# Putting off the feed-forward layer of 896 tokens behind the attention, as Strassen units of 448 tokens

## The chip, the core and the metric

The kernel runs on one core of a Trainium2 chip. The core has a matrix engine (TensorE, PE in the profile; PEld is its weight load), a vector engine (VectorE, DVE), a scalar engine (ScalarE, ACT), a general engine (GpSimd, POOL) and SyncE (SP), which here only issues DMAs. Each engine works through its own instructions in order; semaphores hold them to each other. The metric is the device time of one execution in microseconds (us), lower is better: the median of the runs shown, beside one execution that the hardware profiler recorded.

## What is computed

Softmax attention over 8 batches of 12 heads (448 positions of 64), and then a gated feed-forward layer (FFN) on all 3584 tokens:

```python
scores = scale * np.matmul(q, k.transpose(0, 1, 3, 2))
scores = scores - np.max(scores, axis=-1, keepdims=True)
attn = np.exp(scores)
attn = attn / (np.sum(attn, axis=-1, keepdims=True) + 1e-09)
attn_out = np.matmul(attn, v)
x = attn_out.transpose(0, 2, 1, 3).reshape(B * S, H * D)      # 3584 x 768
g = x @ w_gate                                                # 768 x 1536
silu = g * (1.0 / (1.0 + np.exp(-g)))
val = x @ w_val                                               # 768 x 1536
out = silu * val @ w_out                                      # 1536 x 768
```

All inputs and outputs are float32; the kernel multiplies in float16.

## The kernel before

**Attention.** Heads are taken in pairs (48 pairs, 6 per batch). For a pair, GpSimd's queue loads queries, keys and values, GpSimd copies them into order (L237), and from pair 12 on two DMA transposes on SP's queue (L239, L243) bring queries and keys into `qkT`. The scores of a chunk are matmuls into a PSUM tile `s` (L329; L341 for the chunk that two pairs share), ScalarE takes their exponential into `E` (L349), and 32 matmuls per pair (L420) multiply by the values: `pv_rest` has the first 8 of them, `pv_pieces` the other 24. `pv_close` divides by the sums on DVE (L449, L450), and `turn_x` transposes the result into `X` with two more DMA transposes on SP (L494, L498). `X[kk]` holds the 896 tokens of batches 2kk and 2kk+1; there are two such buffers.

**PSUM.** Three double tiles (`ps_s`) are shared in rotation by scores, gates, output groups and units. Two single tiles (`ps_f`) are shared by attention products, values and plain outputs.

**FFN in steps.** While attention runs, the tokens go through the FFN in blocks: block 2kk has 384 tokens, block 2kk+1 has 512. A block has 12 `Step`s, one per 128 columns of the hidden layer: 6 gate matmuls, tanh on ScalarE (L584), 6 value matmuls, and on DVE two instructions (L610, L616) that write `hts`. `run_single` splits the value product of a lone step into two halves, `run_pair` interleaves two steps.

**Outputs.** Two chunks of 128 tokens make a pair for a seven-product (Strassen) scheme: `out_group` (L679) has 42 matmuls of 192 columns for half of the output columns. Its first half makes three products, which DVE combines (L718 or ScalarE's L720, then L721 and L723); the second half begins with a product that adds to what L723 wrote. DVE prepares the sums of `hts` (`h_sums`). A third chunk of a 384-token block goes plainly, in four parts of 192 columns (L650).

**The visits.** The attention's order is a `plan` of visits. Each has three score chunks and, mostly, the products of one earlier pair. From the visit `base` on, a table says what each does beside them: `(begins, nf, ng, no, ns)` are the block that begins, the number of steps, output groups, plain output parts, and extra sums on DVE. There are 33 visits. If a visit has one group and no step, `around` is set: `run_group_with` puts the attention products inside the group. No entry of the table before sets it.

**Behind the last exponential.** The last four batches' remainder is worked off as Strassen units. Block 5 (512 tokens of batches 4 and 5) goes in units of 256, and batches 6 and 7 in units of 448. A `Unit` takes 256 hidden columns of gate or value and two token halves with seven products of 3 matmuls each (L795); there are 12 units. It needs four sums of weights, made on GpSimd (`weight_sums`, L758 to L761), and four sums of tokens (`token_sums`). `order_of` fixes the order of a run of units by estimated durations. Then come the output groups of block 4 and block 5, the second run of units, one chunk of 128 tokens alone (`single_out`, L1003), and three pairs of groups.

Of the kernel before, what the change touches and what calls it, by code (L numbers as in the profile page):

```python
# [17 lines left out]
NB = 2  # L18
# [46 lines left out]
def kernel(  # L65
# [818 lines left out]
    with tc.manual_schedule():  # L884
# [63 lines left out]
        def add_block(i, visits):  # L948
            if i < B - NB - 1:
                f1, own, n = block(i)  # L950
                fvq.extend(f1)
                kk, c0, hts = own
            else:
                own = None
# [12 lines left out]
            groups.extend(x for t in range(1 + odd) for x in pair_groups(kk, c0, hts, t))  # L967
# [121 lines left out]

        def run_group_with(p0):  # L1090
# [6 lines left out]

        def run_two_groups(inside=None):
            gens = [groups.pop(0)[0]() for _ in range(2)]
            for stage in range(2):  # L1100
                for gen in gens:
                    next(gen)
                if inside and not stage:
                    inside()
# [92 lines left out]
        hts5 = hview(384, 512)  # L1197
        vfree = vraw[:].rearrange("p s h c d -> p (s h c d)")
        VE = 2 * NC * D
        t5 = token_space(vfree[:, 3 * VE :], 256)  # L1200
        for x, (chunks, todo) in enumerate(plan):
# [40 lines left out]
            around = bool(todo) and x > base and VISITS[x - base][1:3] == (0, 1)  # L1242
            for _, p0 in todo if not around else []:
                pv(p0)
                if p0 < XPE:
                    turns.append(p0)
                else:
                    turn_x(p0)
# [22 lines left out]
            else:  # L1271
# [6 lines left out]
                if around:  # L1278
                    run_group_with(todo[0][1])
                elif ng:  # L1280
# [17 lines left out]
                if x == len(VISITS) + base - 6:  # L1298
                    space = raws_all[:, 0 : RL // 2].rearrange("p a t b x -> p (a t b x)")
                    wsum_space(space, 10)  # L1300
# [3 lines left out]
                    wsum_space(vfree, 4)  # L1304
            if x == len(VISITS) + base - 6:
                tsums5 = token_sums(X[KL - 1][:, :, 384:], 256, t5)
            if len(VISITS) + base - 6 <= x < len(VISITS) + base - 2:
                tsums5.pop(0)()
            for u in {len(VISITS) + base - 6: range(4), len(VISITS) + base - 2: range(4, 6)}.get(x, []):
                weight_sums(u)  # L1310
            while turns:
                turn_x(turns.pop(0))
        x5 = X[KL - 1][:, :, 384:]
# [50 lines left out]
        units = {}  # L1364
        items = unit_items(units, lambda u: Unit(u, 256, x5, t5, hts5), 256)
        p0 = NPAIR - 1
        pv_open(p0, True)
        pv_rest(p0)
        pv_quad(p0)
        turn_x(p0)  # L1370

        wsum_space(Eall[:, 4 * NK * 128 : ER * EC], 18)
        wsum_space(attp.tile([128, 2 * S + D], FP16, tag="qkT", name="wsum", bufs=QB), 2)
        for vo in Vts[:4]:
            wsum_space(vo[:].rearrange("p h c d -> p (h c d)"), 1)
        for u in range(6, NFB):
            items[f"W_{u}"] = (POOL_, 3.65, [f"W_{u - 1}"], lambda u=u: weight_sums(u))
# [81 lines left out]
```

## Time and profile before

| | us |
|---|---|
| median of 3 runs (429.52 to 430.11) | 429.69 |
| span of the profiled execution | 428.2 |
| first unit matmul (L795) | 300.98 |
| groups of blocks 4 and 5 end, second run of units begins | 351.35 |
| second run of units ends | 399.72 |
| last group matmul ends | 424.1 |

The page cuts the span into 40 slices of 10.7 us and gives the busy share of each in tenths (9 is 90% or more):

```profile
PE   8999999999999999999999999999999999999996
ACT  6975667556566645546667556568655225545221
POOL 8756543999887583658543885934999000000001
PEclk9999999999999999999999999999999999999999
DMA  9999999999999999999999999823100331000125
```

A busy PE is one whose matmuls are pipelined and whose ends are modelled, so a 9 hides idle time of some tenths of a microsecond; these show in the chain and in the instructions in order of time. The DMA row counts engines that have packets under way, and several queues can share an engine.

### The profile page before, as it was taken

How to read it: one execution, taken by the hardware profiler on the slowest of the kernel's cores; microseconds unless marked ns; L12 is line 12 of the kernel's file. 1: busy time of each engine (PE TensorE's matmuls, PEld its weight loads, DVE VectorE, ACT ScalarE, POOL GpSimd, SP SyncE). 2: the span in 40 equal slices, each digit the busy share in tenths (PEclk: the TensorE clock that was granted, in tenths of full speed). 3: DMA queues.
4: the chain of work that ended last, by engine and by line, in shares of the span. 5: the costliest groups of instructions: out<-in, count | busy, mean ns of one | idle time of the engine just before them, and what ended most of it. 6: DMA issues, size and time to landing. Idle time of an engine off the chain costs nothing.

```text
span 428.2 us, 11621 instructions
## 1 busy us (share of the span) xinstructions
PE 420.5 (98%) x4635; PEld 290.2 (68%) x4635; DVE 267.7 (63%) x642; ACT 245.2 (57%) x395; POOL 233.3 (54%) x358
## 2 busy tenths in 40 slices
PE   8999999999999999999999999999999999999996
PEld 3666656555557777747666677777888995555795
DVE  4666562576758665575545776567777765565663
ACT  6975667556566645546667556568655225545221
POOL 8756543999887583658543885934999000000001
PEclk9999999999999999999999999999999999999999
DMA  9999999999999999999999999823100331000125
GB/s 138 177 200 200 199 173 190 121 169 209 160 138 137 115 146 150 146 136 120 124 151 122 139 149 117 152 45 97 25 1 14 101 99 51 0 0 2 38 76 148
DMA packets 108551, 50.02 MB, mean 117 GB/s; under 512 B 60864, under 2 KB 105232, under 8 KB 108496
## 3 DMA queue, kind: packets, MB, share of 16 engines
q0 software_dynamic: 46944, 24.83, 54.0%
q1 hardware_dynamic: 61408, 24.27, 33.6%
q8 instruction: 36, 0.59, 0.7%
q14 instruction: 19, 0.16, 0.1%
q10 hardware_dynamic: 144, 0.17, 0.1%
HBM read 49.55 MB, written 11.01 MB: 141 GB/s over the span
## 4 chain that ended last, share of the span: by engine, by line
PE 77%; DMA 15%; POOL 4%; DVE 1%; ACT 1%; issue 1%; SPq 0%; POOLq 0%; DVEq 0%
PE og L679 18%; PE gp L557 15%; PE un L795 10%; PE vp L557 9%; PE acc L420 8%; PE ub L795 8%; PE s L329 5%; DMA wv<-in_moe_w_val_dram 4%; DMA qkraw<-in_q_dram 4%; DMA qkraw<-in_k_dram 3%; DMA wg<-in_moe_w_gate_dram 2%; PE op L650 2%; POOL qkraw L200 2%; DMA qkT<-qk 1%; PE s L341 1%; PE op L1003 1%
## 5 line engine op out<-in xcount | busy, mean ns | idle before, releaser
L349 ACT ACTIVATE E<-s 128x896 f16<-128x896 f32 x126 | 106.6, 918 | 40.2 <-PE s L329 28.2
L557 PE MATMUL gp<-X,wg 128*128 128x384 f16 (+1 forms) x360 | 73.9, 347 | 0.0
L237 POOL COPY qk<-qkraw 128x512 f16<-128x512 f16 x72 | 43.7, 649 | 50.8 <-DMA qkT<-qk 48.9
L557 PE MATMUL vp<-X,wv 128*128 128x384 f16 (+3 forms) x360 | 66.7, 321 | 0.1
L610 DVE SCALAR_TENSOR_TENSOR t<-sg,gp 128x384 f32<-128x384 f32 (+1 forms) x60 | 36.3, 607 | 42.5 <-ACT sg L584 42.2
L557 PEld LDWEIGHTS <-wv 128*128 128x128 f16 x462 | 43.8, 98 | 25.8 <-issue 0.3
L640 POOL DMA_DIRECT2D out_dram<-osb x3 | 1.6, 541 | 90.9 <-ACT osb L698 90.9
L177 POOL DMA_DIRECT2D vraw<-in_v_dram x72 | 43.8, 629 | 12.8 <-DVE X L492 6.9
L557 PEld LDWEIGHTS <-wg 128*128 128x128 f16 x360 | 32.8, 98 | 26.1 <-issue 1.9
L584 ACT ACTIVATE sg<-gp 128x384 f32<-128x384 f32 (+1 forms) x60 | 32.1, 537 | 28.8 <-PE gp L557 28.1
L177 POOL DMA_DIRECT2D qkraw<-in_k_dram x70 | 42.4, 619 | 7.7 <-DMA wo<-in_moe_w_out_dram 4.7
L367 ACT ACTIVATE E<-s 112x896 f16<-112x896 f32 x48 | 40.5, 919 | 8.5 <-PE s L359 8.3
L420 PEld LDWEIGHTS <-E 128*128 128x128 f16 (+1 forms) x1152 | 37.4, 96 | 10.9 <-issue 4.7
L679 PEld LDWEIGHTS <-hts 128*128 128x128 f16 x528 | 44.1, 98 | 0.3
L420 PE MATMUL acc<-vo,E 128*128 128x65 f16 (+1 forms) x1152 | 42.3, 192 | 0.7 <-DVE X L492 0.3
L616 DVE SCALAR_TENSOR_TENSOR hts<-t,vp 128x384 f16<-128x384 f32 (+3 forms) x60 | 32.5, 541 | 5.5 <-PE vp L557 1.9
L698 ACT ACTIVATE osb<-og 128x384 f32<-128x384 f32 x22 | 10.8, 491 | 39.4 <-PE og L679 37.5
L200 POOL DMA_DIRECT2D qkraw<-in_q_dram x44 | 29.9, 680 | 5.4 <-DMA vraw<-in_v_dram 1.4
L450 DVE TENSOR_TENSOR xt<-acc,R 128x256 f16<-128x256 f32 x72 | 30.6, 425 | 2.5
L329 PE MATMUL s<-qkT 64*128 64x448 f16 x216 | 30.4, 354 | 0.6 <-DMA qkT<-qk 0.5
L679 PE MATMUL og<-wo,hts 128*128 128x192 f16 x264 | 29.0, 246 | 0.0
L679 PEld LDWEIGHTS <-hsum 128*128 128x128 f16 x300 | 25.5, 98 | 1.0
(180 smaller groups left out, 723.8 us busy)
## 6 DMA issues: line engine op xcount, KB each, us to landing
vraw<-in_v_dram POOLq DMA_DIRECT2D x72, 64.0 KB, 4.9
qkraw<-in_q_dram POOLq DMA_DIRECT2D x41, 112.0 KB, 4.8
qkraw<-in_k_dram POOLq DMA_DIRECT2D x68, 64.0 KB, 4.8
wg<-in_moe_w_gate_dram POOLq DMA_DIRECT2D x8, 288.0 KB, 9.7
wv<-in_moe_w_val_dram POOLq DMA_DIRECT2D x8, 288.0 KB, 10.2
wo<-in_moe_w_out_dram POOLq DMA_DIRECT2D x2, 1152.0 KB, 19.4
out_dram<-osb SPq DMA_DIRECT2D x7, 288.0 KB, 4.1
out_dram<-osb SPq DMA_DIRECT2D x6, 336.0 KB, 3.2
```

The lines of the kernel that those rows point to most:

```text
L177: eng.dma_start(dst[ts(s, 64)], rows)
L200: nc.gpsimd.dma_start(dst, flat.rearrange("h (p c) d -> p h (c d)", c=NC))
L237: nc.gpsimd.tensor_copy(dst.rearrange("p c h d -> p h c d"), src)
L329: nc.tensor.matmul(s[:, hx, 0:S], lhsT=t[ts(hx, 64), ts(c + low(pr, hx), 128)], rhs=t[ts(hx, 64), ds(NC * 128, S)], start=True, stop=True,)
L349: nc.scalar.activation(e[:, 0 : 2 * S].rearrange("p (h q) -> p h q", h=2), s[:, :, 0:S], AF.Exp, scale=sm_scale)
L367: nc.scalar.activation(e[:, :, 0:S], s[0:P, :, 0:S], AF.Exp, scale=sm_scale)
L420: nc.tensor.matmul(acc[:, ts(j, D + 1)], lhsT=e[rows, ds(hx * S + j * 128, 128)], rhs=Vts[pr % NV][rows, hx, col, 0 : D + 1], start=first, ...
L557: nc.tensor.matmul(dst[:, 0:w], lhsT=wslice(kind, self.fb, cb), rhs=X[kk][:, cb, ds(c0 + lo, w)], start=(cb == 0), stop=(cb == NCB - 1),)
L610: nc.vector.scalar_tensor_tensor(self.t1[:, 0:n], self.sg[:, 0:n], 1.0, self.gp[:, 0:n], ALU.add, ALU.mult)
L616: nc.vector.scalar_tensor_tensor(self.hts[:, self.fb, ds(lo, w)], self.t1[:, ds(lo, w)], 0.5 * HS, vp[:, 0:w], ALU.mult, ALU.mult)
L679: nc.tensor.matmul(dst, lhsT=lhs(n), rhs=rhs(n), start=first and n == 0, stop=n == NH - 1, skip_group_check=True)
L795: mm = nc.tensor.matmul(dst, lhsT=lhs[:, n], rhs=rhs[:, n], start=first and n == 0, stop=n == NK - 1, skip_group_check=True,)
```

## The change

The whole of batches 4 and 5 (`X[2]`, 896 tokens) is now put off: `add_block` makes steps for blocks 0 to 3 only, and block 4's entry merely queues block 3's output groups. Behind the last exponential, a function `units_of` makes the items of one run of 448-token units with the single chunk and the three pairs of groups. It is used twice, for batches 4 and 5 and for 6 and 7. The table of visits is dealt out anew:

- visits 2 to 10: block 2's 12 steps in pairs, with four groups of block 1 in visits of their own, wrapped around the attention products (`around`);
- visits 11 to 21: block 3's 12 steps, one per visit but for one visit with two;
- visits 22 to 31: six groups and four plain output parts, and no step. Two of the six groups fall on visits without attention products; a new `run_bare_group` runs these. The other four are wrapped.

The sums of tokens for the middle run are taken in late visits on DVE (`tsums6`, 1344 elements per instruction instead of 768), and those for the last run on GpSimd instead of DVE. Of the weight sums, three units' are issued in the visits (before: six), and nine behind them. A pair whose transposed result would go into an `X` buffer that steps still read is kept in `held` until no step is left.

```diff
         def add_block(i, visits):
-            if i < B - NB - 1:
+            if i < B - 2 * NB:
...
         VISITS = [
-            (2, 2, 0, 0, 2), (0, 2, 0, 0, 3), (0, 1, 1, 0, 0), (0, 2, 0, 0, 0), (0, 1, 1, 0, 0),
-            (0, 2, 0, 0, 0), (0, 1, 1, 0, 0), (0, 2, 0, 0, 0), (0, 1, 1, 0, 0), (3, 2, 0, 0, 1),
-            (0, 2, 0, 0, 1), (0, 1, 1, 0, 0), (0, 0, 0, 1, 0), (0, 2, 0, 0, 0), (0, 0, 0, 1, 0),
-            (0, 1, 1, 0, 0), (0, 0, 0, 1, 0), (0, 2, 0, 0, 0), (0, 0, 0, 1, 0), (0, 2, 0, 0, 0),
-            (4, 2, 0, 0, 1), (0, 2, 0, 0, 1), (0, 1, 1, 0, 0), (0, 1, 0, 0, 0), (0, 1, 1, 0, 0),
-            (0, 1, 0, 0, 0), (0, 1, 1, 0, 0), (0, 1, 0, 0, 0), (0, 1, 1, 0, 0), (0, 1, 0, 0, 0),
-            (5, 0, 0, 1, 0), (0, 0, 0, 2, 0), (0, 0, 0, 0, 0),
+            (2, 2, 0, 0, 2), (0, 2, 0, 0, 3), (0, 0, 1, 0, 0), (0, 2, 0, 0, 0), (0, 2, 0, 0, 0),
+            (0, 0, 1, 0, 1), (0, 2, 0, 0, 0), (0, 0, 1, 0, 0), (0, 2, 0, 0, 0), (0, 0, 1, 0, 0),
+            (0, 2, 0, 0, 0),
+            (3, 1, 0, 0, 0), (0, 1, 0, 0, 0), (0, 1, 0, 0, 0), (0, 1, 0, 0, 0), (0, 1, 0, 0, 0),
+            (0, 1, 0, 0, 0), (0, 2, 0, 0, 0), (0, 1, 0, 0, 0), (0, 1, 0, 0, 0), (0, 1, 0, 0, 0),
+            (0, 1, 0, 0, 0),
+            (4, 0, 1, 0, 1), (0, 0, 0, 1, 1), (0, 0, 1, 0, 0), (0, 0, 0, 1, 2), (0, 0, 1, 0, 1),
+            (0, 0, 1, 0, 1), (0, 0, 0, 1, 1), (0, 0, 1, 0, 0), (0, 0, 0, 1, 0), (0, 0, 1, 0, 0),
+            (0, 0, 0, 0, 0),
         ]
...
+        def run_bare_group():
+            gen = groups.pop(0)[0](True)
+            next(gen)
+            add_sum()
+            next(gen)
+
         def run_group_with(p0):
             gen = groups.pop(0)[0](True, lambda: pv_close(p0, 1))
             next(gen)
             pv_pieces(p0)
             pv_close(p0, 0)
             next(gen)
             turn_x(p0)
...
+                elif fvq and fvq[0].at[0] < p0 // NHP // NB - 1:
+                    held.append(p0)
...
+                elif ng and not nf:
+                    run_bare_group()
...
-            for u in {len(VISITS) + base - 6: range(4), len(VISITS) + base - 2: range(4, 6)}.get(x, []):
+            for _ in range({5: 1, 3: 1, 2: 1, 1: 1}.get(len(VISITS) + base - x, 0)):
+                tsums6.pop(0)()
+            for u in {len(VISITS) + base - 6: range(2), len(VISITS) + base - 2: range(2, 3)}.get(x, []):
                 weight_sums(u)
...
-        units = {}
-        items = unit_items(units, lambda u: Unit(u, 256, x5, t5, hts5), 256)
+        def units_of(kk, t, last):
+            units = {}
+            items = unit_items(units, lambda u: Unit(u, S, X[kk], t, hts), S)
+            pairs = [pair_groups(kk, 0, hts, p, last and p == 2, at=p if last else p % 2) for p in range(3)]
...
+        items, pairs = units_of(KL - 1, t6, False)
         p0 = NPAIR - 1
         pv_open(p0, True)
         pv_rest(p0)
         pv_quad(p0)
         turn_x(p0)
...
+        for u in range(3, NFB):
+            items[f"W_{u}"] = (POOL_, 3.65, [f"W_{u - 1}"], lambda u=u: weight_sums(u))
+        run_items(items)
...
+        for fn in token_sums(X[KL], S, t7, nc.gpsimd):
+            fn()
+        sums.clear()
+        sums.extend(f for pair in pairs[1:] for _, fs in pair for f in fs)
+        run_groups(pairs)
...
+        items, pairs = units_of(KL, t7, True)
         run_items(items)
-        sums.extend(f for pair in final[1:] for _, fs in pair for f in fs)
-        run_groups(final)
+        sums.extend(f for pair in pairs[1:] for _, fs in pair for f in fs)
+        run_groups(pairs)
```

More of the change, by code (lines that the diff above doesn't have):

```diff
@@ L966, in add_block @@
             odd = i % 2 == 0
-            groups.extend(x for t in range(1 + odd) for x in pair_groups(kk, c0, hts, t))
+            groups.extend(x for t in range(1 + odd) for x in pair_groups(kk, c0, hts, t, at=1 - t if i == B - 2 * NB else t))
             if not odd:
@@ L1096, in run_group_with @@
             turn_x(p0)
[L1098 to L1104, printed above, removed]
         def run_budget(budget):
@@ L1241 @@
                 add_block(adds[x], end - x)
-            around = bool(todo) and x > base and VISITS[x - base][1:3] == (0, 1)
+            around = bool(todo) and base < x < base + len(VISITS) and VISITS[x - base][1:3] == (0, 1)
             for _, p0 in todo if not around else []:
@@ L1394, in run_groups @@
                 add_sum()
-        x7 = X[KL]
-        t7 = token_space(xp.tile([128, NCB, NT], FP16, tag="X", name="T")[:].rearrange("p a b -> p (a b)"), S)
-        tsums7 = token_sums(x7, S, t7)
-        first, behind = (pair[0][1] for pair in groups5)
-        first[0]()
-        sums.extend([tsums7[0], *first[1:], *behind, *tsums7[1:]])
-        for pair in [groups] + groups5:
-            run_groups([pair])
-        hts = hview(0, NT)
-        units = {}
-        items = unit_items(units, lambda u: Unit(u, S, x7, t7, hts), S)
+        items, pairs = units_of(KL - 1, t6, False)
@@ L1411 @@
-        ops = []
-        def single_last(half, f):
-            if not f:
-                ops.append(ps_f.tile([128, 512], FP32, tag="f", name="op")[:, 0:OH])
-            single_out(ops[half], KL, 0, hts, 6, half, f)
-        for half in range(2):
-            for f in range(NFB):
-                after = [f"F{f % 2}1_{f // 2 * 2 + 1}", f"O{half}_{f - 1}" if f else f"F10_{NFB - 2 + half}"]
-                items[f"O{half}_{f}"] = (PE_, OH / 2400 + 0.0025, after, lambda half=half, f=f: single_last(half, f))
```

67 lines of the change are left out of this document (34 added, 33 removed).

## The prediction, before the changed kernel was run

> **What bounds the kernel now.** I read the page first: busy times, slices, chain.
>
> ```profile
> span 428.2 us, 11621 instructions
> PE 420.5 (98%) x4635; PEld 290.2 (68%) x4635; DVE 267.7 (63%) x642; ACT 245.2 (57%) x395; POOL 233.3 (54%) x358
> PE 77%; DMA 15%; POOL 4%; DVE 1%; ACT 1%; issue 1%; SPq 0%; POOLq 0%; DVEq 0%
> ```
>
> TensorE (PE) is busy for 98% and has 77% of the chain; the chain's DMA pieces lie before 85 us, ahead of everything that the change touches. So a microsecond of matmul removed is a microsecond won, provided that PE stays packed. Then the chain in order of time (start, length, what), for the places where it is not packed, and for the stages behind the attention.
>
> ```profile
> 113.66 1.11 PE acc L420 x31
> 114.78 1.31 PE gp L557 x6
> 116.74 0.70 DVE t L610
> 117.53 0.70 DVE hts L616
> 118.27 1.11 PE acc L420 x31
> ...
> 330.56 20.79 PE og L679 x252
> 352.10 1.13 PE un L795 x6
> ...
> 399.72 3.58 PE op L1003 x22
> 403.29 20.80 PE og L679 x252
> ```
>
> From 113.66 to 118.27 a visit with one FFN step of 512 tokens takes 4.61 us, and the chain leaves PE: gate, tanh, two VectorE (DVE) instructions, then the next attention product, which needs the bank that they free. PE's own work there is 0.67 (scores) + 0.96 (attention products) + 2.6 (step) = 4.23. The tail shows three group pairs in 20.8, the last 896 tokens' units from 351.35 to 399.72 = 48.4, and the single output in 3.6. Third, the instructions in order of time around one output group:
>
> ```profile
> 260.43 0.38 PE L341 MATMUL s<-qkT 64*64 64x448 f16 x4
> 260.89 2.54 ACT L349 ACTIVATE E<-s 128x896 f16<-128x896 f32 x3 [0.78 <-PE s L341]
> ...
> 262.71 0.66 PE L679 MATMUL og<-E,hts 128*128 128x192 f16 x6
> 263.21 0.66 PE L679 MATMUL og<-E,hsum 128*128 128x192 f16 x6
> 263.41 0.36 DVE L718 TENSOR_SCALAR p<-og 128x192 f32<-128x192 f32 x1 [1.03 <-PE og L679]
> ...
> 264.29 0.36 DVE L723 SCALAR_TENSOR_TENSOR og<-p,og 128x192 f32<-128x192 f32 x1
> ...
> 264.71 0.66 PE L679 MATMUL og<-E,hsum 128*128 128x192 f16 x6
> ```
>
> Here the group's first half ends on PE at 263.70 and its second half can start only at 264.71, after three DVE instructions; an FFN value product (263.70 to 264.67) fills that 1.0 us exactly. Last, SyncE's queue (SP), which issues all DMA transposes:
>
> ```profile
> 113.89 1.22 SPq L243 DMA_TRANSPOSE qkT<-qk  x1
> 115.21 1.22 SPq L239 DMA_TRANSPOSE qkT<-qk  x1
> ```
>
> One transpose occupies it for about 1.3 us, and it runs nearly without pause from 86 to 287 us.
>
> **The change, part by part.** All against the profiled 428.2.
>
> Removed from the attention: block 4, 12 steps of 384 tokens. In the chain two such steps run from 240.20 to 244.1, so 1.95 each: 23.4. Block 4's three output parts of 0.99 go too: 3.0. Together 26.4 off PE before the last exponential. Block 2's four output parts and the ten groups stay, in other visits; their stores (0.5 each on SP) go with them.
>
> Behind the attention: before, from the first unit matmul at 300.98 to the end, 127.2. After, twice (48.4 + 3.6 + 20.8) plus the last stores, 428.2 - 424.1 = 4.1: 149.7. Added: 22.4. The difference of 4.0 is the eighth of block 4's products that the seven-product scheme saves, plus what the 256-token units lost to their smaller size. Packed, the kernel would take 428.2 - 26.4 + 22.4 = 424.2.
>
> Now the waits, for which the new visits have less cover:
>
> (a) One step of 512 tokens per visit, ten visits in a row (block 3). The nearest row is the 4.61 cycle: 4.61 - 4.23 = 0.38 idle, or 0.26 where the scores take 0.79. The new visits split the value product, so the second DVE instruction is half as long, but there are two: about the same chain. I take 0.27 each, 2.7; bounds 0 and 3.8. Before, four visits with one 384-token step idled some 0.2 each, which goes: 0.8. Net 1.9.
>
> (b) Groups wrapped around the attention products (eight visits: four among block 2's, four late). The group takes one of three score tiles, so its first matmul needs the exponential of this visit's first scores. The exponentials start 0.41 after the scores (266.78 to 267.19) and take 0.85 apiece (2.54 for three), so the first is done at 1.26 to 1.36. PE has until then only scores and eight attention products, 0.89 (266.78 to 267.67): 0.35 to 0.47 idle. Before, the whole attention product (0.96) or a gate product stood there. In the middle, the 1.0 us of DVE work is covered by 24 attention products, 0.74 (257.65 to 258.39): 0.25 idle. Behind the waiting matmul stand the rest of the pair's products and the second half; DVE's closing of the pair, ScalarE's copy and the pair's transposes on SP wait for them, none of which PE needs soon. Sum 0.6, bounds 0 (if PE arrives late anyway) and 0.75: 4.8. Two of them follow a visit with an output part, where ScalarE's exponentials and copy (2.54 + 0.33) outlast PE's 2.65; 0.2 more each. Sum 5.2.
>
> (c) Two bare groups, with neither step nor attention product. First half waits until 1.3 with PE done at 0.8; second half waits the whole 1.0. 1.55 each: 3.1; bounds 2 x 1.0 and 2 x 1.9.
>
> (d) Four visits with only an output part: ScalarE is the longer by 0.1 to 0.3; 0.4.
>
> Idle added: 1.9 + 5.2 + 3.1 + 0.4 = 10.6. Span: 424.2 + 10.6 = 434.8.
>
> Edits that I cost at nothing, with their cover. Weight sums on POOL: four adds, 3.65 per unit; three units are done early, and nine follow during units of 48.4/12 = 4.03 each. They start ahead and are faster; cover gone, nine times the shortfall. The last tokens' sums move to POOL: its 384-element adds take 0.91, so 1344 elements are estimated at 3.2, four at 12.7, inside the 24.4 us of single output and groups. Token sums for the middle units sit on DVE at late visits, where 768 elements took 1.26; up to 2.2 each, with DVE busy for about 3.5 of 5. The last one stands ahead of the closing of the last pair; PE then has four unit products before it needs DVE. Holding back pairs 36 and 37 until block 3's steps are done delays only their two transposes each, which are read much later.
>
> SP's queue is moved past nothing, but its visits get shorter. From pair 24's transposes to pair 47's it must issue 94 transposes and 13 stores. At 1.42 per transpose (1.30 and about 1 us more every eighth) and 0.5 per store that is 140 us from 127.05 on, so the last is issued near 266 and lands near 271, 5.3 later (the page's median for qkT). Packed PE wants that tile at 296.0 (when it was read before) - 23.4 - 1.0 - 3.5 (a group now later) = 268. With 8 us of idle before, it comes at 276 and SP is not what it waits for. So these two costs do not add.
>
> The Trainium skill speaks otherwise of this queue: "DMA: Bandwidth & Descriptors", section "Issuing engines are not separate DMA queues", holds the sequencer time of issuing a DMA to be usually small beside the DMA. By that, SP could be left out and only the packed 424.2 plus the idle remains; the 1.3 us rows disagree, so the queue stays among the rivals.
>
> The runs shown have a median of 429.7, 1.5 above this profile. I add 1.5: 436.3.
>
> **Rivals.**
>
> Packed PE (faster). If the waits of (b) to (d) fall where PE is held anyway, or exponentials run further ahead than I think, only Strassen's saving is left: 424.2 + 1.5 = 425.7, and up to 428.8 with 3.1 of idle. Place: the first og matmul in a wrapped group. It decides once idle added is under 4.0. For it: before, ten groups idled nowhere. Against it: in those, an FFN product lay over both waits.
>
> SP's queue sets the pace. The last qkT lands at 271 if all goes well, but at 1.48 per transpose (126 took 202.7 us less 16.3 for stores, pauses included) 5.6 later, and the longest landing took 11.0: 5.7 more, 282. Behind it come one group visit, a score and two attention products, 6.5; units start at 277.5 to 288.8, the end, 149.7 later, is 427 to 438.5, median 428.7 to 440. For it: almost no pause on SP for 200 us. Against it: the tiles of queries and keys landed 6 to 21 us ahead of their first score from 200 us on, and slower visits give time back.
>
> POOL too late. If weight sums stretch from 3.65 to 4.6 beside DVE (one took 1.22 instead of 0.91 per add), nine of them lose 9 x 0.55 = 5 us in the first units: 441. Against: POOL kept 0.91 from 301.99 to 305.58 while units ran.
>
> PE's clock. The granted clock stands at 1.00 in every stretch up to 400 us, with idle of 0.4 in single-step visits. If some twenty new gaps made it drop over the 50 us of late visits, their 43 us of matmul would double: near 480. The Trainium skill ("TensorE: Matmul & The Clock Gate", "A second HAM failure mode: psum-queue depth-cycling") tells of such micro-idles; no row here shows a drop.
>
> **How the numbers follow.** Forecast 0.62 (432 to 441 by its bounds), packed 0.17, SP 0.13, POOL 0.05, clock 0.03. This kernel can be told from no change beyond about 0.2%, 0.9 us: 428.8 to 430.5 is "same". Faster: 0.14 of packed and 0.01 of SP, 0.15. Same: the rest of packed, 0.03, SP's low end 0.02, the forecast's edge 0.03: 0.08. Slower: 0.77. The range reaches from 427.0 into the packed case (0.1 below it) to 441.5 (the forecast's idle at its upper bounds, 14.8, gives 440.5; 0.07 above).
>
> **What would show it.** Right: units start near 285 instead of 300.98 (274.6 if packed); PE idle of 0.3 to 0.5 before og, ended by ACT E, and again at the second half, ended by DVE og L723; 1 us and more in the two bare groups; the two late stretches of units 48.4 each, without idle ended by POOL. Wrong: no idle before og (packed); idle before s ended by DMA qkT (SP); idle before ub or un ended by POOL; clock below 1.00.

## The result and the profile after

The changed kernel takes 451.41 us (median of 4 runs, 449.38 to 454.40); beside it, the kernel before takes 429.61 (429.44 to 430.11). The ratio is 1.0507, with a 95% interval of 1.0486 to 1.0528: 5% slower. The prediction had said slower, but 436.3 with a range up to 441.5. The profiled execution of the changed kernel has a span of 449.5 us where the prediction worked out 434.8, so 14.7 us have to be found. Three executions of two kernels told below (446.30, 448.52 and 1067.77 us, the last the one profiled execution of its kernel) were slowed as a whole and are left out of the times and ratios.

The first fence is from the page of the changed kernel: the span, PE's busy time, PE's busy tenths and granted clock in 40 slices of 11.2 us, and the chain by engine.

```profile
span 449.5 us, 11279 instructions
PE 424.1 (94%) x4485; PEld 280.0 (62%) x4485; DVE 277.8 (62%) x630; ACT 246.1 (55%) x372; POOL 242.7 (54%) x354
...
PE   8999999999998999999999869899998699999996
...
PEclk9999999999999999999999979999999999999999
...
PE 73%; DVE 11%; DMA 6%; POOL 3%; issue 2%; ACT 2%; SPq 1%; DVEq 0%; POOLq 0%; ACTq 0%
```

PE's share fell from 98% to 94%, and VectorE (DVE) has 11% of the chain where it had 1%. PE's row has two dips to 6 before the last slice: the 24th slice (258 to 270 us), where the clock shows a 7 too, and the 32nd (348 to 360). The chain in order of time (start, length, what) shows what stands at the first:

```profile
257.81 0.62 SPq L239
258.53 1.21 SPq L243
259.83 0.54 SPq L640
260.43 4.60 DMA out_dram<-osb
265.21 0.50 ACT osb L698
265.74 0.37 DVE osb L735
...
266.71 2.99 PE og L679 x18
...
271.02 2.14 PE og L679 x24
```

Read it downwards. SyncE's queue (SP) issues two transposes (L239, L243) and only then a store of a finished output part (L640). The store lands at 265. Until then all four output buffers `osb` are taken, so ScalarE (ACT) cannot write the next part (L698), DVE cannot write its half behind it (L735), and PE cannot write scores into the tile that DVE was to empty. After that wait, 18 group matmuls take 2.99 us where 24 take 2.14 a little later.

How late that store is shows in the instructions in order of time (start, length, engine, line; in brackets the idle time before and what ended it), first of the changed kernel, then of the kernel before:

```profile
253.16 0.36 DVE L735 SCALAR_TENSOR_TENSOR osb<-og,p 128x192 f32<-128x192 f32 x1 [1.20 <-ACT osb L698]
254.02 1.83 SPq L494 DMA_TRANSPOSE X<-xt  x1
...
259.83 3.03 SPq L640 DMA_DIRECT2D out_dram<-osb  x4
```

```profile
266.96 0.36 DVE L735 SCALAR_TENSOR_TENSOR osb<-og,p 128x192 f32<-128x192 f32 x1 [0.92 <-ACT osb L698]
...
267.49 2.56 SPq L640 DMA_DIRECT2D out_dram<-osb  x4
```

In the changed kernel the first pair of output chunks is complete at 253.52, and its store is issued 6.3 us later: SP's queue has four transposes (L494, L498, L239, L243) to issue first. In the kernel before it is issued 0.2 us after the pair is complete.

The same view at the second dip, and the tail that answers to the one shown of before:

```profile
341.41 0.76 DVE hts L862
...
347.54 2.98 DVE hsum L542
350.54 2.97 DVE hsum L543
354.29 18.01 PE og L679 x216
...
420.68 3.58 PE op L1005 x22
424.25 20.80 PE og L679 x252
```

The chain stays on DVE from 341.41 to 353.5. The tail is as forecast: 3.58 and 20.80. What runs beside DVE in those 12 us shows in the instructions in order of time:

```profile
341.30 2.73 POOL L994 TENSOR_TENSOR T<-X 128x1344 f16<-128x1344 f16 x1 [19.93 <-PE un L795]
341.41 3.09 DVE L862 SCALAR_TENSOR_TENSOR hts<-silu,kept 128x448 f16<-128x448 f32 x1
...
344.43 0.61 DVE L862 SCALAR_TENSOR_TENSOR hts<-silu,un 128x448 f16<-128x448 f32 x1
...
345.09 2.64 PE L1005 MATMUL op<-wo,hts 128*128 128x384 f16 x14 [1.68 <-DVE hts L862]
...
347.05 3.03 POOL L996 TENSOR_TENSOR T<-X 128x1344 f16<-128x1344 f16 x1
347.54 2.96 DVE L542 TENSOR_TENSOR hsum<-hts 128x768 f16<-128x768 f16 x1
```

GpSimd (POOL) makes the last run's token sums here. A DVE instruction that reads two tensors in SBUF and starts beside one ends about 0.4 us after it: L542 ends at 350.50, POOL's L996 at 350.08. L542 takes 0.55 us otherwise. The L862 that reads `un`, which lies in PSUM, keeps its 0.61.

PE's waits from 121 to 300 us (us in all, times, longest; a fifth, of 0.4 us, is left out), where the profile of before lists none from 121 to 352 us:

```profile
PE s L329 <- DVE osb L735: 4.0, 2, 3.8
PE og L679 <- ACT E L349: 3.8, 8, 0.6
PE og L679 <- DVE og L723: 2.6, 4, 0.8
PE s L329 <- DVE hts L616: 0.8, 5, 0.2
```

The second, third and fourth are waits that the prediction named (under b, c and a). The first is not.

From these views, measured against forecast, by stretch. "Packed" is the profile of before less what left the stretch and plus what came, by the prediction's prices:

| stretch | packed | forecast idle | measured | lost beyond the forecast |
|---|---|---|---|---|
| first scores of pair 21 to those of pair 30 (from 129.0) | 52.9 | 2.4 | 57.3 | 2.0 |
| to the first scores of pair 39 | 49.1 | 2.7 | 52.0 | 0.2 |
| to the first unit matmul (293.3) | 43.6 | 5.5 | 55.0 | 5.9 |
| to the second run's first unit matmul (372.1) | 72.8 | 0 | 78.8 | 6.0 |
| to the end (449.5) | 76.9 | 0 | 77.4 | 0.5 |

(52.9 = 63.3 - 4 x 2.6 for four steps that are not there yet; 49.1 = 57.4 + 4 x 2.6 - 4 x 1.95 - 2 x 3.47 - 4 x 0.99; 43.6 = 51.3 - 8 x 1.95 + 2 x 3.47 + 0.99, with 3.47 a sixth of the 20.8 of six groups. The start of both kernels, up to 129.0, is equal.) Two stretches hold 11.9 of the 14.7.

### The profile page after: what moved, and what is told of

The parts are those of the page before. It is cut to its first block, busy times and chain, and to the rows that moved or that the text cites. A ratio compares the mean times of both kernels' runs of the same rounds, so it can differ in the third digit from the quotient of the medians.

```text
span 449.5 us, 11279 instructions
## 1 busy us (share of the span) xinstructions
PE 424.1 (94%) x4485; PEld 280.0 (62%) x4485; DVE 277.8 (62%) x630; ACT 246.1 (55%) x372; POOL 242.7 (54%) x354
## 4 chain that ended last, share of the span: by engine, by line
PE 73%; DVE 11%; DMA 6%; POOL 3%; issue 2%; ACT 2%; SPq 1%; DVEq 0%; POOLq 0%; ACTq 0%
PE og L679 15%; PE gp L557 14%; PE un L795 11%; PE ub L795 8%; PE vp L557 7%; PE acc L420 6%; PE s L329 3%; DMA qkT<-qk 3%; DMA vraw<-in_v_dram 2%; PE acc L385 2%; PE op L650 2%; DVE t L610 1%; POOL qkraw L200 1%; PE s L359 1%; DVE hts L616 1%
## 5 line engine op out<-in xcount | busy, mean ns | idle before, releaser
L237 POOL COPY qk<-qkraw 128x512 f16<-128x512 f16 x72 | 45.4, 672 | 44.4 <-DMA qkT<-qk 42.1
L557 PE MATMUL gp<-X,wg 128*128 128x384 f16 (+1 forms) x288 | 60.8, 353 | 0.0
L610 DVE SCALAR_TENSOR_TENSOR t<-sg,gp 128x384 f32<-128x384 f32 (+1 forms) x48 | 29.5, 620 | 40.5 <-ACT sg L584 29.6
L557 PEld LDWEIGHTS <-wv 128*128 128x128 f16 x408 | 38.9, 98 | 20.6 <-DVE xt L450 0.8
L557 PE MATMUL vp<-X,wv 128*128 128x384 f16 (+3 forms) x288 | 50.7, 311 | 0.5 <-DVE xt L450 0.4
L640 POOL DMA_DIRECT2D out_dram<-osb x3 | 1.6, 539 | 90.3 <-ACT osb L698 90.3
L177 POOL DMA_DIRECT2D vraw<-in_v_dram x72 | 44.1, 638 | 10.4 <-DVE t L610 7.4
L679 PEld LDWEIGHTS <-hts 128*128 128x128 f16 x528 | 45.3, 99 | 5.2 <-issue 4.4
L420 PEld LDWEIGHTS <-E 128*128 128x128 f16 (+1 forms) x1152 | 38.6, 97 | 10.8 <-issue 5.3
L420 PE MATMUL acc<-vo,E 128*128 128x65 f16 (+1 forms) x1152 | 44.0, 194 | 0.9 <-DVE X L492 0.3
L698 ACT ACTIVATE osb<-og 128x384 f32<-128x384 f32 x22 | 10.8, 491 | 53.3 <-PE og L679 46.8
L557 PEld LDWEIGHTS <-wg 128*128 128x128 f16 x288 | 25.9, 98 | 21.7 <-issue 1.5
L584 ACT ACTIVATE sg<-gp 128x384 f32<-128x384 f32 (+1 forms) x48 | 26.0, 548 | 18.4 <-PE gp L557 17.5
L679 PE MATMUL og<-wo,hts 128*128 128x192 f16 x264 | 29.4, 248 | 3.9 <-ACT E L349 3.8
L679 PEld LDWEIGHTS <-hsum 128*128 128x128 f16 x300 | 25.8, 99 | 7.5 <-issue 3.5
L679 PE MATMUL og<-E,hsum 128*128 128x192 f16 x216 | 23.7, 249 | 6.3 <-DVE og L723 4.2
## 6 DMA issues: line engine op xcount, KB each, us to landing
wv<-in_moe_w_val_dram POOLq DMA_DIRECT2D x8, 288.0 KB, 10.4
```

Source lines behind the costliest of these rows:

```text
L177: eng.dma_start(dst[ts(s, 64)], rows)
L237: nc.gpsimd.tensor_copy(dst.rearrange("p c h d -> p h c d"), src)
L420: nc.tensor.matmul(acc[:, ts(j, D + 1)], lhsT=e[rows, ds(hx * S + j * 128, 128)], rhs=Vts[pr % NV][rows, hx, col, 0 : D + 1], start=first, ...
L557: nc.tensor.matmul(dst[:, 0:w], lhsT=wslice(kind, self.fb, cb), rhs=X[kk][:, cb, ds(c0 + lo, w)], start=(cb == 0), stop=(cb == NCB - 1),)
L610: nc.vector.scalar_tensor_tensor(self.t1[:, 0:n], self.sg[:, 0:n], 1.0, self.gp[:, 0:n], ALU.add, ALU.mult)
L679: nc.tensor.matmul(dst, lhsT=lhs(n), rhs=rhs(n), start=first and n == 0, stop=n == NH - 1, skip_group_check=True)
```

## The experiments

The theory: (1) the store behind transposes on SP's queue, and the clock that drops after PE's wait, cost 5 to 6 us before the units; (2) POOL's four long additions cost 6 us between the two runs of units, by holding DVE. Rivals: that units and groups of 448 tokens are slower by themselves; that token sums from POOL are late; that wrapped groups, bare groups and single-step visits cost more than forecast; that the long wait only takes up slack.

**The token sums back on DVE.**

```diff
-        for fn in token_sums(X[KL], S, t7, nc.gpsimd):
-            fn()
+        tsums7 = token_sums(X[KL], S, t7)
+        first, behind = (pair[0][1] for pair in pairs[1:])
         sums.clear()
-        sums.extend(f for pair in pairs[1:] for _, fs in pair for f in fs)
+        first[0]()
+        sums.extend([tsums7[0], *first[1:], *behind, *tsums7[1:]])
```

> The changed kernel with one part undone: the last run's four token sums are issued to DVE between the groups, as before the change, and not to POOL. Theory A (POOL's long additions hold the DVE additions that have two SBUF inputs): the DVE groups L862 hts<-silu,kept and L541 to L543 fall from 1.9 to 3.1 us back to 0.55 to 0.65, the PE waits for hts and hsum of 1.6 to 1.8 us go, the stretch from the first unit matmul to the second run's start falls from 78.9 to 73 us, and the time from 451.4 to about 445.5 us (443.5 to 447.5). Rival B (units and groups of 448 tokens are slower for a reason of their own): that stretch stays at 77 to 80 us and the time moves by less than 1 us. Rival C (DVE has no room): the token sums of some 1.5 us each on DVE bring waits of their own, and the time stays above 449 us.

Measured: 443.53 us (442.32 to 443.87), ratio 1.0315 (1.0281 to 1.0349). From the first unit matmul to the second run's it takes 72.97 us; the prediction's sum had 72.8. Theory A holds, rivals B and C fall. On DVE the four sums take 0.85 to 0.86 us each, as they do in the profile of before.

**The same, with POOL adding for nobody.** POOL makes four additions of the same shapes into the first run's sum space, which is free by then.

```diff
+        for fn in token_sums(X[KL], S, t6, nc.gpsimd):
+            fn()
         tsums7 = token_sums(X[KL], S, t7)
```

> As the run before it, with the token sums on DVE, and besides POOL makes four additions of the same shapes into the first run's sum space, which nobody reads. Theory A (it is POOL's running beside DVE that costs): the DVE additions are stretched to 2 to 3 us again, and the stretch from the first unit matmul to the second run's start is 76 to 82 us, 3 to 9 us above the run without POOL's additions; the time is 449 to 454 us. Rival B (what cost was that the token sums, or what hung on them, came late from POOL): nobody waits for these additions, so the time is that of the run without them, within 1 us.

Measured: 448.50 us (448.10 to 452.23), ratio 1.0455 (1.0403 to 1.0507), 5.0 us above the run without them. The stretch takes 75.98, 3.0 more. Both stand just below theory A's lower ends (449 and 76) and far from rival B's 1 us. The instructions in order of time:

```profile
346.04 3.04 POOL L997 TENSOR_TENSOR vraw<-X,qkraw 128x1344 f16<-128x1344 f16 x1
346.53 2.96 DVE L542 TENSOR_TENSOR hsum<-hts 128x768 f16<-128x768 f16 x1
...
349.55 0.67 PE L679 MATMUL og<-E,hsum 128*128 128x192 f16 x6 [1.84 <-DVE hsum L542]
```

Nobody reads what POOL writes, and at this place DVE and PE stand as long as in the changed kernel. So it is POOL's running that costs, not a late result. The other 2 us of the 5 are from before the units: the `osb` wait was 5.4 us in this profile and 4.3 in the one without POOL's additions. In the changed kernel the stretch lost 6.0 and not 3.0; POOL began there 0.8 us after the last `un` matmuls had begun (341.30 and 340.48) and here 3.2 us before them (337.47 and 340.63), so it met fewer of DVE's group sums here. That this explains the other 3 us was not tried by itself.

**The kernel before, with only its last token sums on POOL.**

```diff
-        tsums7 = token_sums(x7, S, t7)
+        for fn in token_sums(x7, S, t7, nc.gpsimd):
+            fn()
...
-        sums.extend([tsums7[0], *first[1:], *behind, *tsums7[1:]])
+        sums.extend([*first[1:], *behind])
```

> The kernel before with nothing changed but the last run's four token sums, moved from DVE to POOL as the change does. Theory A (POOL's long additions hold DVE's additions and multiplications of two SBUF inputs, and PE's groups wait for these): DVE instructions of two SBUF inputs beside the four POOL additions take 1.5 to 3 us, PE waits of 1 to 2 us on hsum or og appear in the groups, and the time rises from 429.4 to between 432 and 436 us. Rival B (the additions only hurt in the changed kernel, where they meet the first run's last hts): the time stays within 1 us of 429.4.

Measured: 435.45 us (435.32 to 436.62), ratio 1.0137 (1.0115 to 1.0160): 5.5 us slower. The stretch from the first unit matmul to the second run's grew from 50.2 to 56.3 us. The instructions in order of time at the largest of the new waits:

```profile
339.60 3.04 POOL L995 TENSOR_TENSOR T<-X,T 128x1344 f16<-128x1344 f16 x1
...
340.24 2.81 DVE L540 TENSOR_TENSOR hsum<-hts 128x768 f16<-128x768 f16 x1
...
343.42 0.36 DVE L723 SCALAR_TENSOR_TENSOR og<-p,og 128x192 f32<-128x192 f32 x1
...
343.84 1.14 PE L679 MATMUL og<-E,qkraw 128*128 128x192 f16 x6 [2.58 <-DVE og L723]
```

Here PE does not even wait for the sum that POOL holds (L540), but for the short L721 and L723 queued behind it. PE's listed waits in this stretch are 4.0 us in all (2.6, 1.0 and 0.4). Most of the rest is the clock: after the wait of 2.58 us the granted clock is 0.50 (344 to 346 us), and 18 group matmuls take 2.86 us where 1.5 is usual. Theory A holds; rival B falls.

**The token sums on POOL, each in three pieces.** With the late stores on POOL's queue as in a run told below (439.55 us with the sums on DVE).

```diff
-        for fn in token_sums(X[KL], S, t7, nc.gpsimd):
-            fn()
+        for c in range(NK):
...
+            nc.gpsimd.tensor_sub(t1, b12, b11)
+            nc.gpsimd.tensor_sub(t2, b22, t1)
+            nc.gpsimd.tensor_sub(t3, b22, b12)
+            nc.gpsimd.tensor_sub(t4, b21, t2)
```

> The changed kernel with the late stores on POOL's queue, and the last run's token sums left on POOL, but each addition of 1344 elements cut in three of 448, so twelve short ones and not four long. Theory A (a DVE instruction with two SBUF inputs stands until the POOL addition that has begun is over, and runs then): beside the pieces, each of some 1.1 us, DVE's instructions take at most 1.6 us and not 3.1, PE's waits on hts and hsum are 0.3 to 1 us each and not 1.6 to 1.8, the stretch from the first unit matmul to the second run's start is 74 to 77 us (73.1 without any POOL sums, 78.8 with whole ones), and the time is 440.5 to 443.5 us. Rival B (the two engines share a bandwidth, and what counts is the number of elements): the DVE additions are stretched by the same total, the stretch is 78 to 80 us and the time 444.5 to 446.5 us.

Measured: 439.56 us (439.46 to 439.88), ratio 1.0202 (1.0136 to 1.0268; the runs of before beside it spread from 428.70 to 433.88). The stretch takes 73.5 us, even less than theory A's 74 to 77, the time is 0.9 below its lower end, and PE's waits of a microsecond are gone. In order of time:

```profile
337.98 1.34 POOL L1430 TENSOR_TENSOR T<-X,T 128x448 f16<-128x448 f16 x1
338.46 1.27 DVE L542 TENSOR_TENSOR hsum<-hts 128x768 f16<-128x768 f16 x1
339.28 1.35 POOL L1427 TENSOR_TENSOR T<-X 128x448 f16<-128x448 f16 x1
```

DVE's L542 ends at 339.73, again 0.4 after the POOL addition that had begun before it, and the next POOL addition takes 1.35 instead of 1.03. So each engine stands for one instruction of the other; with pieces of a microsecond that fits into what PE has to do. The same 5376 elements are added on POOL, so rival B falls.

**The late stores on ACT's queue.** This and the next three runs ask about the first dip. The stores of all 33 visits of the table move here; the token sums stay on POOL.

```diff
+                out_queues[0] = (nc.scalar,)
...
-    def store(osb, kk, l0, n, m0, w, queues=(nc.sync,), large_first=False):
+    def store(osb, kk, l0, n, m0, w, queues=None, large_first=False):
+        queues = queues or out_queues[0]
```

> The changed kernel with the output stores of the attention's last visits issued on ACT's queue and not on SP's, where they stand behind the transposes. Theory A (a store late behind transposes holds osb, osb holds DVE, DVE holds PE, and PE's clock falls after that): the PE wait of 3.76 us at 262 us goes, the granted clock of 260 to 280 us is above 0.95 and not 0.83, the first unit matmul comes at 286 to 288.5 us and not 293.3, and the time falls by 5 to 7 us to 444.5 to 446.5. Rival B (the lost time before the units is the sum of many short waits in the groups, of single-step visits, and the long wait only takes slack): the first unit matmul comes within 1.5 us of 293.3. Rival C (ACT, waiting for DVE's half of a part before it issues a store, makes exponentials late): new waits on E of 1 us and more, the time 449 us and above.

Measured: 471.86 us (469.09 to 475.31), ratio 1.0989 (1.0914 to 1.1065): rival C, and far above its 449. The `osb` wait is gone, but ACT's exponentials wait 20.6 us in all for stores, four times. In order of time, ACT's queue at the longest, and PE:

```profile
157.88 6.88 ACTq L643 DMA_DIRECT2D out_dram<-osb  x5
...
164.80 2.54 ACT L349 ACTIVATE E<-s 128x896 f16<-128x896 f32 x3 [6.95 <-DMA out_dram<-osb]
...
165.77 4.00 PE L557 MATMUL gp<-X,wg 128*128 128x384 f16 x12 [6.23 <-ACT E L349]
```

The exponentials stand behind the stores in ACT's order, and PE behind the exponentials. Why five parts take 6.88 us to issue here, when four took 2.6 to 3.0 on SP, stays open. The run says nothing for or against the theory of the `osb` wait.

**The late stores left out.** With the sums on DVE; the output rows that leave in the last 11 visits are not written.

```diff
+                out_queues[0] = (None if x >= base + 22 else nc.sync,)
...
+        if queues[0] is None:
+            return
```

> The run with the token sums back on DVE (443.5 us), and besides the output stores of the last 11 visits of the attention (all that leave from block 4's first scores on) are left out, so those rows are not written; everything else is computed. Theory A (a store behind transposes on SP's queue is what holds osb, DVE and at last PE near 262 us, and the idle then costs PE its clock): the wait of 4.3 us on osb L735 goes, the granted clock of 262 to 272 us is 1.00 and not 0.83, the first unit matmul comes at 285 to 287 us and not 291.8, and the time is 436.5 to 439 us. Rival B (the wait only shows slack that another engine, DVE's closing of the pair or SP's transposes, would show in its place): another wait of 2 us or more stands near 262 us and the time is 441 us or more.

Measured: 439.32 us (439.04 to 439.88), ratio 1.0220 (1.0204 to 1.0236), 4.2 us less than with the stores (443.53). The first unit matmul comes at 286.85 and not 291.84, inside theory A's 285 to 287; the time is 0.3 above its upper end. The stretch from 262 to 272 us (length, then busy time of PE, PE's weight loads, DVE, ACT, POOL; PE's granted clock, DMA share, GB/s), first of the changed kernel, then of this run:

```profile
262.00:272.00 10.00, 6.24 (x68) 5.51 (x65) 3.00 (x10) 2.92 (x4) 1.08 (x1) 0.66 0.59 149
```

```profile
262.00:272.00 10.00, 9.11 (x143) 7.73 (x144) 7.19 (x19) 7.00 (x11) 6.10 (x8) 1.00 0.60 92
```

68 matmuls at a clock of 0.66 against 143 at 1.00. The clock does not drop where the wait is not. Rival B falls: no other wait took its place (the longest is 0.8). Whether a fifth `osb` buffer would do as much was not tried.

**A later pair's transposes behind the visit's stores on SP.** With the sums on DVE; in the last 11 visits a later pair's copies and transposes are issued behind the visit's group.

```diff
-                        prep(p)
+                        if x >= base + 22:
+                            later_preps.append(p)
+                        else:
+                            prep(p)
...
+            while later_preps:
+                prep(later_preps.pop(0))
```

> The run with the token sums back on DVE (443.5 us), and in the last 11 visits the copies and transposes of a later pair are issued behind the visit's output group and not ahead of it, so that the stores of a visit stand before its transposes on SP's queue. Theory A (only the order of stores and transposes on SP matters): no wait on osb, first unit matmul at 285.5 to 288 us, 437 to 440 us. Rival B (the transposes have no room to be late): waits on DMA qkT of 2 us and more at the scores, time 443 us or above. Rival C (it is not the order but the few osb buffers, all full at once): the osb wait shrinks by less than half.

Measured: 443.04 us (439.11 to 445.17), ratio 1.0295 (1.0239 to 1.0351): not to be told from 443.53. The wait near 262 us went, but PE waits 2.1 us for `osb` at 280, behind the next pair's store, and now 1.0 for a transpose. The edit changes less than it seems to: the first pair, complete at 253.0, is stored at 258.1, still behind three transposes, the two moved ones of the visit before among them. So half of the wait went and part of it came back as rival B has it; a store that truly leaves at once on SP's queue was not tried.

**The late stores on POOL's queue.** With the sums on DVE; the same edit as for ACT, with `nc.gpsimd`, for all 33 visits.

> The run with the token sums back on DVE (443.5 us), and the output stores of the attention's visits of the last three blocks are issued on POOL's queue. Theory A (freeing the stores from the transposes is enough, and POOL has slack): the osb wait goes, first unit matmul at 286 to 288.5, 437.5 to 440.5 us. Rival B (POOL waits for the output part before each store, and its copies and with them the transposes and scores come late, as ACT's exponentials did when the stores stood on its queue): waits on DMA qkT, 445 us or more.

Measured: 439.55 us (438.98 to 440.07), ratio 1.0223 (1.0206 to 1.0241); the first unit matmul at 287.0, as with the stores left out. Theory A holds. PE's waits from 121 to 300 us (L682, L726 and L738 are L679, L723 and L735 in this kernel's lines):

```profile
PE og L682 <- ACT E L349: 4.2, 9, 0.6
PE og L682 <- DVE og L726: 2.6, 4, 0.8
PE s L329 <- DVE hts L616: 0.8, 5, 0.2
PE s L329 <- DVE osb L738: 0.3, 1, 0.3
```

What is left are the waits that the prediction had named. By the table's stretches this run loses 3.6, 2.9 and 5.9 us against packed, 12.4 in all; the forecast was 10.6.

**No wrapping, twice.** The attention's product ahead of the output group in all eight wrapped visits: once in the changed kernel as it is, once with sums on DVE and stores on POOL.

```diff
-            around = bool(todo) and base < x < base + len(VISITS) and VISITS[x - base][1:3] == (0, 1)
+            around = False
```

> The changed kernel with the attention's product of a visit issued ahead of its output group, and not inside it: the groups of visits without a feed-forward step stand bare. Theory A (the wrapped groups wait for the first scores' exponentials and for DVE, 5 us in all): the units start 2 to 5 us earlier than 293.3 and the time falls to 446.5 to 449.5 us. Rival B (a bare group behind the product waits as long for its own DVE sum, and the product for the exponential): no change within 1.5 us. Rival C (the wrapping hides more than it costs): slower by 1 to 4 us.

> The run with the token sums on DVE and the late stores on POOL (439.55 us), with the attention's product issued ahead of the group in all eight wrapped visits. With the osb wait out of the way this shows the wrapping alone. Theory A (a bare group waits 0.84 us for its own DVE sum instead of 0.4 to 0.6 for an exponential, so wrapping is worth 0.2 to 0.5 us in each of eight visits): 441 to 443.5 us. Rival B (no difference): 439 to 440.5 us. Rival C (wrapping costs): below 438.5 us.

Measured: the first 452.52 us (449.46 to 453.21), ratio 1.0515 (1.0468 to 1.0563), the same as the changed kernel; the second 443.32 (442.16 to 446.36), ratio 1.0327 (1.0283 to 1.0372), 3.8 above 439.55. In both, the groups' wait for DVE's L723 (L726 in the second's lines) grows from 2.6 to 10.0 and 10.4 us and that for exponentials falls to 1.2. In the first, the `osb` wait fell from 4.0 to 2.3 at the same time and the mean granted clock rose from 0.992 to 0.996 (it stays at 1.00 behind that wait, and falls to 0.54 to 0.61 from 140 to 144 us, behind a group's wait of 2.41); that this hides the loss is argued. The second run, which has no `osb` wait and a clock of 1.00 from 120 to 360 us, shows it: wrapping is worth some 4 us (its theory A). A wrapped group idles 0.4 to 0.6 for its exponential where a packed PE would not, but a bare one idles more.

**Block 3's steps in pairs, and the early groups beside steps.** Both with sums on DVE and stores on POOL.

```diff
-            (3, 1, 0, 0, 0), (0, 1, 0, 0, 0), (0, 1, 0, 0, 0), (0, 1, 0, 0, 0), (0, 1, 0, 0, 0),
+            (3, 2, 0, 0, 0), (0, 0, 0, 0, 0), (0, 2, 0, 0, 0), (0, 0, 0, 0, 0), (0, 2, 0, 0, 0),
...
```

> The run with the token sums on DVE and the late stores on POOL (439.55 us), with block 3's twelve steps in pairs, two in one visit and none in the next, and not one in each of ten visits. Theory A (a visit with a single step idles 0.42 us, 4.69 against PE's own 4.27, and a pair of steps does not): that goes, and the visits without a step lose less than 0.8 us each, since exponentials run ahead: 436.5 to 439 us. Rival B (a visit without any step is set by ScalarE's three exponentials, 2.54 and a start of 0.4, against PE's 1.7, and five of them lose 1 us and more each): 440 to 444 us.

```diff
-            (2, 2, 0, 0, 2), (0, 2, 0, 0, 3), (0, 0, 1, 0, 0), (0, 2, 0, 0, 0), (0, 2, 0, 0, 0),
+            (2, 2, 0, 0, 2), (0, 2, 0, 0, 3), (0, 1, 1, 0, 0), (0, 2, 0, 0, 0), (0, 1, 1, 0, 0),
...
```

> The run with the token sums on DVE and the late stores on POOL (439.55 us), with the first 22 of the last 33 visits dealt out otherwise: block 2's four output groups each beside one step of block 2, as before the change (nine visits instead of eleven), then block 3's steps one per visit over twelve visits, and a visit with an output part. Theory A (four early groups wrapped around attention products lose 0.6 to 1.1 us each, of which waits on exponentials of 1.9 us and on DVE of 0.6 are listed): these waits go, the first scores of pair 39 come 2 to 4 us earlier than 238.3 less what two more single-step visits lose (0.4 each), and the time is 436.5 to 438.5 us. Rival B (what is saved there is lost again, because every visit then has less PE work than ScalarE's exponentials and the two DVE instructions need): 439 to 441 us.

Measured: pairs 440.34 us (440.14 to 440.36), ratio 1.0239 (1.0222 to 1.0256), inside rival B's range, 0.8 above 439.55 with intervals that overlap; the waits on `hts` went and 2.3 us of scores waiting for exponentials came. Groups beside steps: 438.24 and 439.55 us, ratio 1.0207 (1.0186 to 1.0227), 438.9 us by it, between theory A's upper end and rival B's lower one, so it decides for neither; there is no trace of it that could say where its time goes. Two other ways to deal this work out leave the time about where it was; that the reason is less FFN work beside the same exponentials is argued, not shown.

No kernel tried here beats the one before. The best of this design that write every output row, at 438.9 to 439.6 us, are 9 to 10 us behind it.

## Why the prediction was wrong

- **Direction and packed sum: right.** With both unforeseen costs gone, the stretch of the first units and groups takes 73.14 us (sums on DVE) and 73.5 (in pieces on POOL) against 72.8; the second units, single output and groups took 48.5, 3.6 and 20.8 in the changed kernel, as forecast. The saving of 4.0 us is there, and is spent many times over.
- **(a) Single-step visits: right in size.** 2.7 were added for ten such visits; the stretch that holds them lost 2.9.
- **(b) Wrapped groups, (c) bare groups, (d) output parts: right in kind, somewhat small in the early part.** The waits on the exponentials are 0.4 to 0.6, the bare groups' second wait 0.84. In the late part 5.9 us were lost with the stores out of the way, against 5.5. In the early part 3.6 in that run (4.4 in the changed kernel), against 2.4: listed in the changed kernel are four waits on exponentials of 1.9 in all, one of 0.6 for DVE's sum and one of 0.4 of a value product; the rest was not followed up.
- **"The last tokens' sums move to POOL: ... inside the 24.4 us of single output and groups": the first step that failed.** Their length was right (2.73 to 3.04 against 3.2) and they did fit. What was not costed is what they do to DVE meanwhile. Costed at nothing, it was 6.0 us in the changed kernel and 5.5 in the kernel before with nothing else changed (there some 1.5 of it by the clock). The profile of before had the signs. The prediction took "768 elements took 1.26" as a price, though three additions of that kind took 0.55 there and only one 1.26. And the instructions of before in order of time held this pair:

```profile
253.01 1.22 POOL L237 COPY qk<-qkraw 128x512 f16<-128x512 f16 x2
...
253.65 0.99 DVE L540 TENSOR_TENSOR qkraw<-hts 128x768 f16<-128x768 f16 x1
```

POOL's copies end at 254.23 and DVE's addition at 254.64, again 0.4 later. With additions of 3 us in the place of copies of 0.6, the same rule gives the 2.96.

- **SP's queue, "So these two costs do not add": the second step that failed.** The transposes went as worked out: the last `qkT` landed at 271.8, and PE waited for none. (The longest landing, given as 11.0, is that of L239; L243's was 12.2. Nothing came of it.) But the queue was examined for that one customer. Its other load is stores, and these give back the four `osb` buffers. With a group or an output part in every late visit and no step between, a store that stands 6.3 us behind four transposes holds `osb`, DVE and PE: 3.8 us, and the clock after it some 2 more. "Stores 0.5 each" was the price of issuing them, not of their coming late.
- **PE's clock.** The rival expected many short gaps to make it drop over 50 us. It did drop, but after the one long wait, and for a few us: 18 group matmuls took 2.99 where the later 24 would give 1.6, and 24 attention products 1.32 (269.70) where 0.84 is usual, so some 2 us. The gaps of 0.4 to 0.8 left it at 1.00 throughout. The Trainium skill ("TensorE: Matmul & The Clock Gate", "Part 1: The HAM clock gate") has the clock fall to half after an idle window of about 3.4 us; this trace agrees with the half (0.50 from 266 to 270 us), behind 3.76 us of wait. Other runs differ from it in the length: waits of 2.58 us (the kernel before with sums on POOL) and 2.41 (the first run without wrapping) brought the same drop, so here gaps shorter than the skill's cost the clock.
- **POOL too late: did not occur.** No unit matmul waited for POOL's weight sums.

The two failed steps lie in the stretches that lost 5.9 + 6.0 of the 14.7; the early part, the tail and rounding make the rest. Without them the kernel is at 439.55 us (stores on POOL, sums on DVE) and 439.56 (sums in pieces) against the forecast 436.3, and inside the range.

## What to carry to other kernels

When work moves to an idle engine, cost it on the engine beside it as well: long POOL additions in SBUF stand in DVE's way instruction by instruction, and cutting them short (here in three) removes the loss where moving them back also would. When a queue is checked, check it for every customer: a store that only gives a buffer back is as urgent as the next write into that buffer, and when visits get shorter, the buffers turn over faster while the queue does not. And before matmul work is taken out from between exponentials, ask what else will cover their latency: here 4 us saved in matmuls cost 12 us of gaps that the dealings-out tried here did not get rid of.

## What the runs showed of the hardware that was not expected

- A DVE instruction with two SBUF inputs that meets a POOL addition ends about 0.4 us after it, whether the addition takes 3.0 or 1.3 us (0.55 us alone; 2.96 and 1.27 beside it). With one input in PSUM it is not held (0.61). POOL is held too: 1.03 us becomes 1.34, 2.73 becomes 3.04. The Trainium skill ("SBUF — State Buffer", "SBUF: two separate sides") says that the port pair which the two engines share is locked for a whole instruction and not divided; the runs with long and with cut additions agree.
- PE's granted clock, from 120 to 360 us in the profiles of the runs above, fell to 0.50 behind every wait of PE of 2.41 us and more (2.41, 2.58, 3.76, 4.31, 5.44 and three longer than 4 with the stores on ACT's queue) and behind none of 2.35 and less. By the clock in windows of 2 us it stayed low for 3.4 us in three profiles (sums on DVE, the kernel before with sums on POOL, no wrapping) and for 6.8 in the changed kernel and where POOL added for nobody.
- The same four additions took 0.85 to 0.86 us each on DVE and 2.73 to 3.04 on POOL: the idle engine was three times as slow, and held the busy one meanwhile.
- Stores on ACT's queue stopped its exponentials for up to 6.95 us; on POOL's queue the same stores cost nothing that these profiles show (POOL was busy for 47.9 of 52 us in the middle stretch, against 35.3).
